# Where the sums of the second weights are formed, and how the last block is stored

## The chip, the cores and the metric

The kernel runs on one core of a Trainium2 chip. The metric is the device time of that core in microseconds, the median of several executions. The engines are named as in the profile: PE (TensorE, matmuls), PEld (its weight loads), DVE (VectorE), ACT (ScalarE), POOL (GpSimd) and SP (SyncE, which here only issues DMAs). Each works through its own instructions in order and waits on semaphores of the others.

## The reference, cut to what matters

A linear attention with a decaying state gives 3072 tokens of 512 numbers. A mixture of experts follows: all 8 experts run on all tokens, and each expert's output is weighted per token by a matrix `P` that 8 rounds of Sinkhorn normalisation make.

```
for e in range(E):                       # 8 experts
    h = np.maximum(x @ w1[e], 0.0)       # 3072x512 @ 512x1024
    ye = h @ w2[e]                       # 3072x1024 @ 1024x512
    out += P[:, e:e + 1] * ye
```

The product `h @ w2[e]` and the sum over the experts are the part that the change touches. It is the last stage of the program, from about 1119 us on.

## The kernel before, in words

The attention comes first, then stage A (`x @ w1`, with relu), then stage B (`h @ w2`). Both products are computed in 2x2 blocks with seven block products instead of eight (Winograd's form of Strassen's scheme). They are named M1 to M7. For seven products, the kernel needs sums of blocks as operands beside the blocks themselves: on the side of `h` stage A has stored them in DRAM (`hd`), on the side of `w2` they are formed in stage B, once per expert.

Every operand is split for precision into a rounded part in float32r and the rest (operand minus rounded part). A block product then takes three matmuls: rounded by rounded, rest by rounded, rounded by rest. ACT makes the rounded part (`hi_act`, L77), DVE makes the rest (`lo`, L80).

**Units and rows.** Stage B has 24 units, `UnitB(n, e, r)`: 8 experts (in falling order) by 3 blocks `r` of 1024 tokens. The list `ROW` sets the order of the block products. One row of the program is: M6 of unit n, M1 of unit n+1, M3 of n, M7 of n, M2 of n+1, M5 of n+1, M4 of n. So M1 is the second product of a row, M2 the fifth, M5 the sixth, M4 the seventh. A product is four parts (`q` = 0 to 3) of six matmuls (`mm`, L551), so a row is 28 parts or 168 matmuls. The rows of one expert are three: its first, its second and its third.

**What a part issues.** `b_part(s)` issues part s: the six matmuls; after a product's last part `post(i)`, which is a copy on ACT (M1, M5, M6; L579) or an output block on DVE (`emit`, for M2, M3, M7, M4: a sum with a stored copy, L562, and a product with `P`, L564; for M4 only the product, L560); then the loads of blocks of `h` that a place has come free for (`h_load`, L611, on SP); then the conversion of the `h` block of part s+5 (`h_conv`: ACT rounds, DVE makes the rest). Since six buffers hold the rounded parts, that conversion waits until PE has left part s-1. The third matmul of a part is the first to read the rest.

**Outputs.** The first expert's blocks are stored by SP (L567). All later ones are added to DRAM by a DMA with `accum_op=ALU.add`, which POOL issues (L569).

**Second weights.** For each change of expert, seven in all, `w2_tasks` prepares the next expert's `w2` in two halves f = 0 and 1. A half is: a load of 1 MB to the buffer `RW` (`w2_load`, L622, on SP); four subtractions 128x512 in that buffer (`tt`, L652, on POOL), which make the operands of M5, M6, M4 and M7; then three times a rounding (`hi`, ACT) and a rest (`rest`, DVE), for 3, 2 and 2 of the seven operands. The results go to the one of the tiles `X0` and `X1` that the running expert does not read. Both halves stand in one list `bq`, filled after the first part of the expert's first row. In three of four parts one entry is taken from it:

```
            if q != 1:
                run(bq, 1)
            if g == 0 and i == M6 and q == 0 and e + 1 < E:
                bq.extend(w2_tasks(e + 1, 0) + w2_tasks(e + 1, 1))
```

So the load of half 0 falls into the row's first product, its four subtractions go to POOL in M3 and M7, and its rests to DVE in M2 and M5. The load of half 1 comes in M4, its subtractions in M1 and M3 of the second row. The new operands are first read in M1 of the third row.

Of the kernel before, what the change touches and what calls it, by code (L numbers as in the profile page):

```python
# [12 lines left out]
ALU = mybir.AluOpType  # L13
# [4 lines left out]
N, DM, E, F = B * S, H * D, 8, 1024  # L18
# [7 lines left out]
NPAIR = CPB // 2  # L26
# [11 lines left out]
M1, M2, M3, M4, M5, M6, M7 = range(7)  # L38
PRE = [M1, M2, M5]
# [4 lines left out]
VP = {M1: 0, M2: 1, M3: 2, M7: 3, M5: 4, M6: 5, M4: 6}  # L44
# [3 lines left out]
def kernel(  # L48
# [17 lines left out]
    pe, act, dve, pool = nc.tensor, nc.scalar, nc.vector, nc.gpsimd  # L66
    sp = nc.sync
# [5 lines left out]
    def rd(t):  # L73
        return t.bitcast(F32)

    def hi_act(o, i):
        act.activation(o, i, AF.Copy)  # L77

    def lo(eng, o, full, h):
        eng.tensor_tensor(o, full, rd(h), ALU.subtract)  # L80
# [23 lines left out]
    def run(q, n):  # L104
        for _ in range(min(n, len(q))):
            q.pop(0)()
# [72 lines left out]
    class UnitA:  # L179
# [22 lines left out]
        def post(self, i):  # L202
            t = self.t
            ps = PS1[self.bank[i]]
            s1, s5, u2, c12 = [TMP[:, k, :] for k in range(4)]
            if i == M1:
                act.activation(s1, ps, AF.Copy)
            elif i == M5:
                act.activation(s5, ps, AF.Copy)
            elif i == M6:  # L210
                act.activation(u2, ps, AF.Copy)
            elif i == M3:
                dve.tensor_tensor(c12, ps, u2, ALU.add)  # L213
                dve.scalar_tensor_tensor(self.new("S3"), c12, 0.0, t["A11"], ALU.max, ALU.subtract)
                self.store("S3", M7)
            elif i == M7:
                o = self.new("A22")
                dve.tensor_tensor(o, ps, s5, ALU.add)  # L218
                act.activation(o, o, AF.Relu)  # L219
                self.store("A22", M4)  # L220
                self.new("S1")
                self.new("S2")
            elif i == M2:
                o = self.new("A11")
                dve.tensor_tensor(o, ps, s1, ALU.add)  # L225
                act.activation(o, o, AF.Relu)  # L226
                self.store("A11", M1)
            elif i == M4:
                act.activation(self.new("A12"), ps, AF.Relu)  # L229
                self.store("A12", M2)  # L230
# [23 lines left out]
    with tc.manual_schedule():  # L254
        with ExitStack() as ph:
# [156 lines left out]
            for tau in range(2, NCHUNK):  # L412
                c, b = divmod(tau, B)
# [107 lines left out]
        def place(s):  # L521
            return HX[s - 8] if 8 <= s < 12 else HL[(s if s < 8 else s - 4) % NHL]

        def follows(s):
            u = s - 4 - NHL
            return u if u < 8 else u + 4
        WB = [X1, X0]
        YS = [OT[:, 10:12, :], XSC[:, 0:2, :], XSC[:, 2:4, :]]
        TB = [OT[:, 2 * k:2 * k + 2, :] for k in range(3)]
        PB = [XSC[:, 2:4, :]] + [OT[:, 6 + 2 * k:8 + 2 * k, :] for k in range(2)]  # L530
        y_n = [0]

        class UnitB:
# [37 lines left out]
            def post(self, i):  # L571
                ps = self.pieces(i)
                s1, s5, u2 = TB
                if self.n == 0:
                    s1 = YS[1]

                def copy(o):
                    for d, t in ps:
                        act.activation(o[:, d], t, AF.Copy)  # L579

                if i == M1:
                    copy(s1)
                elif i == M5:
                    copy(s5)
                elif i == M6:
                    copy(u2)
                elif i == M2:
                    self.emit(0, 0, ps, s1)
                elif i == M3:
                    self.emit(0, 1, ps, u2)  # L590
                elif i == M7:
                    self.emit(1, 1, ps, s5)
                elif i == M4:
                    self.emit(1, 0, ps, None)

            def load_p(self):
                src = pd.rearrange("(e m) s -> e m s", e=E)[self.e, 8 * self.r:8 * self.r + 8, :]
# [3 lines left out]
        UB = [UnitB(n, e, r) for n, (e, r) in enumerate((e, r) for e in reversed(range(E)) for r in range(NPAIR))]  # L601
# [6 lines left out]
        def h_load(s):  # L608
            if s < len(parts):
                u, i, q = parts[s]  # L610
                sp.dma_start(rd(place(s)), hd[u.e][u.r][i][:, q, :])  # L611

        def h_conv(s):
            if s < len(parts):
                hi, low = HH[s % NHH], place(s)
                hi_act(hi, rd(low))
                lo(dve, low, rd(low), hi)

        w2x = RW.rearrange("p (s c) -> p s c", s=7)

        def w2_load(e, f):
            sp.dma_start(w2x[:, 0:4, :], w2[E - 1 - e, f])  # L622
# [15 lines left out]
        w2t = [(M5, M7, M1), (M6, M3, M5), (M4, M2, M6), (M7, M7, M3)]  # L638
# [10 lines left out]

        def w2_tasks(e, f):  # L650
            def tt(o, a, b):
                return lambda: pool.tensor_tensor(w2x[:, VP[o]], w2x[:, VP[a]], w2x[:, VP[b]], ALU.subtract)  # L652

            def hi(a, b):
                t = WB[e % 2][:, a:b, :, f * 512:(f + 1) * 512]
                hi_act(t[:, :, 0], w2x[:, a:b])

            def rest(a, b):
                t = WB[e % 2][:, a:b, :, f * 512:(f + 1) * 512]
                lo(dve, t[:, :, 1], w2x[:, a:b], t[:, :, 0])  # L660

            q = [lambda: w2_load(e, f)] + [lambda: None] * 6
            q += [tt(*x) for x in w2t]
            for a, b in ((0, 3), (3, 5), (5, 7)):
                q += [lambda a=a, b=b: hi(a, b), lambda a=a, b=b: rest(a, b)]
            return q

        bq = []

        nload = [NHL + 4]  # L670

        def b_part(s):
            u, i, q = parts[s]
            if i == M6 and q == 0 and u.n + 1 < len(UB):
                UB[u.n + 1].load_p()
            u.mm(i, q, (HH[s % NHH], place(s)))
            if q == QE - 1:
                u.post(i)
            if s >= 4:
                while follows(nload[0]) <= s:  # L680
                    h_load(nload[0])
                    nload[0] += 1
                h_conv(s + 5)
            e, g = divmod(u.n, NPAIR)
            if q != 1:
                run(bq, 1)
            if g == 0 and i == M6 and q == 0 and e + 1 < E:
                bq.extend(w2_tasks(e + 1, 0) + w2_tasks(e + 1, 1))


        x_load(X1, 1)
# [10 lines left out]
        for n, u in enumerate(UA):  # L702
# [16 lines left out]
            for m, (k, i) in enumerate(ROW):  # L719
                w = (u, v)[k]  # L720
                if w is not None:
                    w.mm(i)
                    w.post(i)
                if m == 0 and carry is not None:
                    carry.last_sum()
                if m == 4:
                    u.sums()
                if m in (0, 1, 5):
                    run(wq, 1)
                if m in (1, 6) or n >= NJ:  # L730
                    run(xq, 2 if n >= NJ else 1)
                for f, x in w2_plan.get((n, m), ()):
                    w2_first(f, x)
                if n == NUA - 2 and m in (5, 6):
                    h_conv(m - 5)
                if n == NUA - 1:
                    for x in {1: (0, 1), 4: (2, 3)}.get(m, ()):
                        b_part(x)
                    for x in {1: (2,), 3: (3,), 4: (4,), 5: (5,)}.get(m, ()):
                        h_conv(x)  # L740
# [8 lines left out]
            h_load(s)  # L749
        for s in range(6, 9):  # L750
            h_conv(s)
        for s in range(4, len(parts)):
            b_part(s)

# [50 lines left out]
```

## Time and profile before

| | |
|---|---|
| median of 3 runs | 2079.45 us (2075.53 to 2083.27) |
| the profiled execution | 2079.61 us |
| its span, first to last instruction | 2077.1 us |
| PE busy | 1992.0 us, 96% of the span |
| DVE busy | 1549.1 us, 75% |
| ACT busy | 1042.0 us, 50% |
| POOL busy | 499.5 us, 24% |
| mean granted TensorE clock | 0.984 |
| stage B: first and last matmul start | 1119.3 and 2066.1 us |

The shares are averages over three stages with different limits. For a change to stage B they say little. What counts there is which wait holds up PE and at what places.

### The profile page before, as it was taken

To read this page: it belongs to the slowest core of one execution; us is meant where nothing else is said; L and a number is where in the kernel's file an instruction comes from. 1 tells how busy PE (TensorE), PEld (TensorE's weight loads), DVE (VectorE), ACT (ScalarE), POOL (GpSimd) and SP (SyncE) were. 2 spreads that over 40 slices of the span, in tenths; PEclk is the share of its full clock that TensorE was granted. 3 is DMA by queue.
4 is the path that set the end of the run, shared out by engine and by line. 5 is a ranking of instruction groups with operands and counts; after the bars stand their busy time and mean duration, and the time that the engine had idled before them with its cause. 6 is when DMAs were issued, how large, how long until landed. Compare 5 with 4: busy or idle time off the path is not lost.

```text
span 2077.1 us, 28831 instructions
## 1 busy us (share of the span) xinstructions
PE 1992.0 (96%) x9273; PEld 1647.7 (79%) x9273; DVE 1549.1 (75%) x2025; ACT 1042.0 (50%) x1668; POOL 499.5 (24%) x479
## 2 busy tenths in 40 slices
PE   7888999998899999999999999999999999999997
PEld 6786877887688888888887887887878787787886
DVE  6795988995666666666677787869687877869765
ACT  3342554553444444444445655555555565555553
POOL 4462433431212111211123101212031112203001
PEclk9898999999999999999999999999999999999999
DMA  7755776776566666666677989999999999999987
GB/s 238 245 168 172 242 247 200 247 249 195 187 216 226 219 221 218 232 214 221 215 248 252 314 269 278 274 276 264 265 293 257 280 275 271 276 284 256 269 266 157
DMA packets 252904, 503.61 MB, mean 242 GB/s; under 512 B 27792, under 2 KB 40400, under 8 KB 250704
## 3 DMA queue, kind: packets, MB, share of 16 engines
q1 hardware_dynamic: 240656, 457.73, 65.5%
q0 software_dynamic: 12096, 44.05, 11.6%
q8 instruction: 72, 1.18, 0.3%
q14 instruction: 80, 0.66, 0.1%
HBM read 268.79 MB, written 232.88 MB: 242 GB/s over the span
## 4 chain that ended last, share of the span: by engine, by line
PE 81%; DVE 6%; issue 5%; DMA 5%; SPq 1%; ACT 1%; POOL 0%; POOLq 0%; DVEq 0%; ACTq 0%
PE psA L190 41%; PE psA L551 21%; PE psB L551 16%; DMA WA<-hd 3%; DVE WA L80 2%; DVE QL L80 1%; PE ps_s L327 1%; SPq L112 1%; DVE X L80 1%; PE ps_x L363 1%; DMA RW<-w 1%; PE psA L372 1%; PE ps_t L339 1%; PE ps_x L358 1%; DVE ta L330 0%
## 5 line engine op out<-in xcount | busy, mean ns | idle before, releaser
L190 PE MATMUL psA<-X,WA 128*128 128x512 f32 x4032 | 932.2, 393 | 23.8 <-DVE OT L213 18.2
L190 PEld LDWEIGHTS psA<-X,WA 128*128 128x128 f32 x4032 | 762.4, 190 | 188.9 <-DVE OT L213 20.3
L551 PE MATMUL psA<-WA,X 128*128 128x512 f32 x2296 | 535.9, 390 | 10.6 <-DVE WA L80 10.1
L77 ACT ACTIVATE WA<-WA 128x512 fp32r<-128x512 f32 x668 | 402.4, 629 | 256.4 <-PE psB L551 109.9
L551 PEld LDWEIGHTS psA<-WA,X 128*128 128x128 f32 x2296 | 429.8, 188 | 106.1 <-DVE WA L80 16.8
L80 DVE TENSOR_TENSOR WA<-WA,WA 128x512 fp32r<-128x512 f32 x487 | 352.3, 767 | 103.4 <-ACT WA L77 97.4
L551 PE MATMUL psB<-WA,X 128*128 128x512 f32 x1728 | 405.1, 390 | 9.1 <-DVE WA L80 6.1
L551 PEld LDWEIGHTS psB<-WA,X 128*128 128x128 f32 x1728 | 324.4, 188 | 79.8 <-DVE WA L80 9.1
L158 POOL TENSOR_TENSOR RW<-RW 128x256 f32<-128x256 f32 x244 | 227.8, 944 | 633.5 <-DMA RW<-w 364.5
L80 DVE TENSOR_TENSOR WA<-RW,WA 128x768 fp32r<-128x768 f32 x122 | 145.3, 1192 | 52.6 <-ACT WA L77 52.3
L219 ACT ACTIVATE OT<-OT 128x512 f32<-128x512 f32 x96 | 60.7, 632 | 244.9 <-DVE OT L218 244.9
L80 DVE TENSOR_TENSOR WA<-WA 128x512 fp32r<-128x512 f32 x181 | 138.8, 794 | 36.9 <-ACT WA L77 35.1
L569 POOL DMA_DIRECT2D out<-XSC x57 | 49.5, 868 | 475.1 <-DVE XSC L564 259.5
L213 DVE TENSOR_TENSOR OT<-psA,OT 128x512 f32<-128x512 f32 x96 | 66.2, 690 | 106.8 <-PE psA L190 106.8
L77 ACT ACTIVATE WA<-RW 128x768 fp32r<-128x768 f32 x122 | 109.4, 946 | 23.0 <-POOL RW L158 13.9
L225 DVE TENSOR_TENSOR OT<-psA,OT 128x512 f32<-128x512 f32 x96 | 66.2, 690 | 59.1 <-ACT OT L219 52.0
L652 POOL TENSOR_TENSOR RW<-RW 128x512 f32<-128x512 f32 x56 | 88.0, 1577 | 60.1 <-DVE WA L80 29.2
L229 ACT ACTIVATE OT<-psA 128x512 f32<-128x512 f32 x96 | 57.4, 598 | 73.6 <-PE psA L190 43.9
L579 ACT ACTIVATE OT<-psA 128x512 f32<-128x512 f32 x96 | 57.4, 598 | 73.2 <-PE psA L551 69.3
L236 DVE TENSOR_TENSOR OT<-OT 128x512 f32<-128x512 f32 x96 | 91.5, 954 | 3.3
L226 ACT ACTIVATE OT<-OT 128x512 f32<-128x512 f32 x96 | 60.7, 633 | 65.3 <-DVE OT L225 65.3
L240 DVE TENSOR_TENSOR OT<-OT 128x512 f32<-128x512 f32 x96 | 70.1, 730 | 30.3 <-ACT OT L229 26.3
(114 smaller groups left out, 1502.3 us busy)
## 6 DMA issues: line engine op xcount, KB each, us to landing
hd<-OT SPq DMA_DIRECT2D x672, 256.0 KB, 2.6
WA<-hd SPq DMA_DIRECT2D x668, 256.0 KB, 6.0
RW<-w SPq DMA_DIRECT2D x61, 512.0 KB, 4.4
out<-XSC POOLq DMA_DIRECT2D x57, 512.0 KB, 8.1
RW<-w SPq DMA_DIRECT2D x16, 1024.0 KB, 8.3
out<-OT POOLq DMA_DIRECT2D x27, 512.0 KB, 8.1
OT<-pd SPq DMA_DIRECT2D x23, 512.0 KB, 7.0
raw<-kT SPq DMA_DIRECT2D x24, 256.0 KB, 3.8
```

The lines of the kernel that those rows point to most:

```text
L77: act.activation(o, i, AF.Copy)
L80: eng.tensor_tensor(o, full, rd(h), ALU.subtract)
L158: eng_add.tensor_tensor(x[:, WP[o]], x[:, WP[p]], x[:, WP[q]], op)
L190: pe.matmul(ps, w[:, a, k * P:(k + 1) * P], x[:, b, k * 512:(k + 1) * 512], start=i in PRE and k == 0 and m == 0, stop=k == 1 and m == 2, ...
L213: dve.tensor_tensor(c12, ps, u2, ALU.add)
L219: act.activation(o, o, AF.Relu)
L225: dve.tensor_tensor(o, ps, s1, ALU.add)
L226: act.activation(o, o, AF.Relu)
L236: dve.tensor_tensor(t["S2"], t["S1"], t["A11"], ALU.subtract)
L240: dve.tensor_tensor(self.new("S4"), self.t["A12"], self.t["S2"], ALU.subtract)
L551: pe.matmul(ps[d] if isinstance(ps, tuple) else ps[:, d, :], w[:, a, q * 256 + d * P:q * 256 + d * P + P], h[b], start=i in PRE and q == 0 ...
L652: return lambda: pool.tensor_tensor(w2x[:, VP[o]], w2x[:, VP[a]], w2x[:, VP[b]], ALU.subtract)
```

## The change

Three things are changed, all in stage B.

- The four subtractions of a half are issued on DVE instead of POOL. One stands behind each part of the second product (M1) of a row: half 0 in the expert's first row, half 1 in the second.
- Roundings and rests no longer come from a list that is emptied entry by entry. They stand at fixed parts: rounding and rest of the first three operands behind the first part of M5, then rounding, rest and rounding behind its other three parts, and the last rest behind the first part of M4. The load of half 1 is issued behind the second part of M4 in the first row, the load of half 0 for the next change of expert behind the first part of the third row; the very first one ahead of the loop.
- The last output block of the program (M4 of the last unit) is not accumulated by POOL. SP loads the running sum of that block to `TB[0]`; DVE multiplies each half by `P` and adds the loaded half; SP stores each half.

```diff
+                elif i == M4 and self.n < len(UB) - 1:
+                    self.emit(1, 0, ps, None)
                 elif i == M4:
-                    self.emit(1, 0, ps, None)
+                    o = out[2 * self.r + 1, 0].rearrange("p (d t) -> p d t", d=2)
+                    sp.dma_start(TB[0], o)
+                    for d in range(2):
+                        y, t = YS[0][:, d], [t for x, t in ps if x.start <= d < x.stop][0]
+                        dve.tensor_tensor(y, t[:, d % t.shape[1]], PB[1 + self.n % 2][:, 1, :], ALU.mult)
+                        dve.tensor_tensor(y, y, TB[0][:, d], ALU.add)
+                        sp.dma_start(o[:, d], y)
...
-                return lambda: pool.tensor_tensor(w2x[:, VP[o]], w2x[:, VP[a]], w2x[:, VP[b]], ALU.subtract)
+                return lambda: dve.tensor_tensor(w2x[:, VP[o]], w2x[:, VP[a]], w2x[:, VP[b]], ALU.subtract)
...
-            q = [lambda: w2_load(e, f)] + [lambda: None] * 6
-            q += [tt(*x) for x in w2t]
-            for a, b in ((0, 3), (3, 5), (5, 7)):
-                q += [lambda a=a, b=b: hi(a, b), lambda a=a, b=b: rest(a, b)]
-            return q
+            t = [tt(*x) for x in w2t]
+            h = [lambda a=a, b=b: hi(a, b) for a, b in ((0, 3), (3, 5), (5, 7))]
+            r = [lambda a=a, b=b: rest(a, b) for a, b in ((0, 3), (3, 5), (5, 7))]
+            return {(f, M1, x): [t[x]] for x in range(4)} | {
+                (f, M5, 0): [h[0], r[0]], (f, M5, 1): [h[1]], (f, M5, 2): [r[1]], (f, M5, 3): [h[2]],
+                (f, M4, 0): [r[2]]}
...
-            e, g = divmod(u.n, NPAIR)
-            if q != 1:
-                run(bq, 1)
-            if g == 0 and i == M6 and q == 0 and e + 1 < E:
-                bq.extend(w2_tasks(e + 1, 0) + w2_tasks(e + 1, 1))
+            e, g = divmod(u.n - (i in PRE), NPAIR)
+            if u.n >= (i in PRE) and e + 1 < E:
+                if (g, i, q) == (0, M6, 0):
+                    w2p.clear()
+                    w2p.update(w2_tasks(e + 1, 0) | w2_tasks(e + 1, 1))
+                for f in w2p.get((g, i, q), ()):
+                    f()
+                if (g, i, q) == (0, M4, 1):
+                    w2_load(e + 1, 1)
+                if (g, i, q) == (2, M6, 0) and e + 2 < E:
+                    w2_load(e + 2, 0)
...
+        w2_load(1, 0)
         for s in range(4, len(parts)):
             b_part(s)
```

On DVE, this is the difference in the second product of an expert's first row (here the second expert's; `WA` tiles hold blocks of `h`, `RW` the loaded weights; L661 is the subtraction's line in the changed kernel):

```order
-L80 TENSOR_TENSOR WA0_71<-WA0_71,WA2_1774 128x512 x3
-L80 TENSOR_TENSOR WA0_71<-WA0_71,WA1_72 128x512
+L80 TENSOR_TENSOR WA0_71<-WA0_71,WA2_1774 128x512
+L661 TENSOR_TENSOR RW_73<-RW_73 128x512
+L80 TENSOR_TENSOR WA0_71<-WA0_71,WA2_1774 128x512
+L661 TENSOR_TENSOR RW_73<-RW_73 128x512
+L80 TENSOR_TENSOR WA0_71<-WA0_71,WA2_1774 128x512
+L661 TENSOR_TENSOR RW_73<-RW_73 128x512
+L80 TENSOR_TENSOR WA0_71<-WA0_71,WA1_72 128x512
+L661 TENSOR_TENSOR RW_73<-RW_73 128x512
```

The four subtractions now stand one by one between the rests of four parts of `h`; on POOL they are gone, and only the accumulating stores are left there.

On DVE in the fifth to seventh product of the same row (`X1` is the tile that takes the next expert's operands, L562 and L564 are the output block of M2):

```order
+L562 TENSOR_TENSOR OT_1775<-psB1_4774,OT_1775 128x1024
+L564 TENSOR_TENSOR OT_1775<-OT_1775 128x1024
+L80 TENSOR_TENSOR WA0_71<-WA0_71,WA1_72 128x512 x2
 L80 TENSOR_TENSOR X1_1773<-RW_73,X1_1773 128x3x512
-L562 TENSOR_TENSOR OT_1775<-psB1_4774,OT_1775 128x1024
-L564 TENSOR_TENSOR OT_1775<-OT_1775 128x1024
-L80 TENSOR_TENSOR WA0_71<-WA0_71,WA1_72 128x512 x2
+L80 TENSOR_TENSOR WA0_71<-WA0_71,WA1_72 128x512
+L80 TENSOR_TENSOR WA0_71<-WA0_71,WA2_1774 128x512
 L80 TENSOR_TENSOR X1_1773<-RW_73,X1_1773 128x2x512
-L80 TENSOR_TENSOR WA0_71<-WA0_71,WA1_72 128x512
-L80 TENSOR_TENSOR WA0_71<-WA0_71,WA2_1774 128x512
```

The three rests of the weights (to `X1`) moved behind M2's output block and behind two more rests of `h`.

On DVE at the end of the program (`psA` holds M4 of the last unit):

```order
 L562 TENSOR_TENSOR XSC_74<-psA1_254,OT_1775 128x512
 L564 TENSOR_TENSOR XSC_74<-XSC_74,OT_1775 128x1024
-L560 TENSOR_TENSOR XSC_74<-psA0_253,OT_1775 128x512
-L560 TENSOR_TENSOR XSC_74<-psA1_254,OT_1775 128x512
+L601 TENSOR_TENSOR OT_1775<-psA0_253,OT_1775 128x512
+L602 TENSOR_TENSOR OT_1775<-OT_1775 128x512
+L601 TENSOR_TENSOR OT_1775<-psA1_254,OT_1775 128x512
+L602 TENSOR_TENSOR OT_1775<-OT_1775 128x512
```

Two instructions became four. On SP's queue a load of `out` stands behind the last load of `h`, and two stores behind it.

## Rows read from the trace of the kernel before

**Rows 1.** Waits in stage B: engine and line <- releaser: us, times, longest.

```profile
POOL RW L652 <- DMA RW<-w: 28.7, 7, 22.4
PEld psA L551 <- DVE WA L80: 16.8, 15, 1.9
PE psA L551 <- DVE WA L80: 10.1, 13, 1.5
PEld psB L551 <- DVE WA L80: 5.9, 4, 1.9
PE psB L551 <- DVE WA L80: 4.5, 3, 1.5
```

**Rows 2.** Windows: stretch, length, PE busy (x matmuls), clock, DMA share, GB/s.

```profile
1186.00:1256.00 70.00, 70.00 (x311) 1.00 0.86 287
1256.00:1304.00 48.00, 45.46 (x199) 1.00 0.94 264
...
1846.00:1894.00 48.00, 45.54 (x198) 1.00 0.96 272
```

**Rows 3.** Timeline, a first row: start, us, engine, instructions [idle before <- releaser].

```profile
1281.22 2.55 DVE L80 TENSOR_TENSOR WA<-WA 128x512 fp32r<-128x512 f32 x1
...
1281.58 5.04 POOL L652 TENSOR_TENSOR RW<-RW 128x512 f32<-128x512 f32 x3
...
1283.69 3.48 DVE L80 TENSOR_TENSOR WA<-WA,WA 128x512 fp32r<-128x512 f32 x2
...
1289.55 4.35 DVE L80 TENSOR_TENSOR WA<-WA,WA 128x512 fp32r<-128x512 f32 x4
...
1290.29 1.66 PE L551 MATMUL psA<-WA,X 128*128 128x512 f32 x6 [0.24 <-DVE WA L80]
1290.54 1.59 POOL L652 TENSOR_TENSOR RW<-RW 128x512 f32<-128x512 f32 x1
...
1292.74 4.38 PE L551 MATMUL psA<-WA,X 128*128 128x512 f32 x18 [0.80 <-DVE WA L80]
...
1293.82 1.75 DVE L80 TENSOR_TENSOR X<-RW,X 128x1536 fp32r<-128x1536 f32 x1
...
1298.61 3.70 PE L551 MATMUL psA<-WA,X 128*128 128x512 f32 x15 [1.49 <-DVE WA L80]
```

**Rows 4.** Timeline of a third row, without work on weights.

```profile
1348.61 1.29 DVE L80 TENSOR_TENSOR WA<-WA 128x512 fp32r<-128x512 f32 x2 [2.74 <-ACT WA L77]
...
1369.02 11.04 PE L551 MATMUL psA<-WA,X 128*128 128x512 f32 x48
...
1370.48 1.23 DVE L564 TENSOR_TENSOR XSC<-XSC,OT 128x1024 f32<-128x1024 f32 x1
1371.62 2.49 DVE L80 TENSOR_TENSOR WA<-WA,WA 128x512 fp32r<-128x512 f32 x4
...
1375.81 2.70 DVE L80 TENSOR_TENSOR WA<-WA,WA 128x512 fp32r<-128x512 f32 x4 [1.70 <-ACT WA L77]
...
1379.90 4.47 PE L551 MATMUL psB<-WA,X 128*128 128x512 f32 x19
```

**Rows 5.** Timeline of DVE in a second row, beside POOL's subtractions.

```profile
1310.95 4.83 DVE L80 TENSOR_TENSOR WA<-WA,WA 128x512 fp32r<-128x512 f32 x4 [2.31 <-ACT WA L77]
```

**Rows 6.** The loads of the second weights, L622.

```profile
DMA to landing us min/median/max: 5.8/8.3/10.4
```

**Rows 7.** Timeline of the program's end.

```profile
2062.87 0.86 POOL L569 DMA_DIRECT2D out<-XSC  x1 [4.58 <-DVE XSC L564]
2065.88 1.37 DVE L560 TENSOR_TENSOR XSC<-psA,OT 128x512 f32<-128x512 f32 x2 [3.31 <-PE psA L551]
2067.55 0.86 POOL L569 DMA_DIRECT2D out<-XSC  x1 [3.81 <-DVE XSC L560]
```

**Rows 8.** Landings of POOL's accumulating stores, L569.

```profile
DMA to landing us min/median/max: 5.3/8.1/10.6
```

**Rows 9.** The page's DMA issues: count, KB each, us to landing.

```profile
hd<-OT SPq DMA_DIRECT2D x672, 256.0 KB, 2.6
```

More of the change, by code (lines that the diff above doesn't have):

```diff
@@ L660, in rest @@
                 lo(dve, t[:, :, 1], w2x[:, a:b], t[:, :, 0])
-            q = [lambda: w2_load(e, f)] + [lambda: None] * 6
-            q += [tt(*x) for x in w2t]
-            for a, b in ((0, 3), (3, 5), (5, 7)):
-                q += [lambda a=a, b=b: hi(a, b), lambda a=a, b=b: rest(a, b)]
-            return q
-        bq = []
+            t = [tt(*x) for x in w2t]
[4 more added lines that the diff above has]
+                (f, M4, 0): [r[2]]}
+        w2p = {}
         nload = [NHL + 4]
```

## The prediction

> **What bounds the kernel now.** I read the waits of stage B first. PE waits there for one thing only, DVE's line 80, the rests: 10.1 + 4.5 us in 16 waits, and its weight loads for the same line 16.8 + 5.9 us [rows 1]. So DVE is late at some places; where, the windows show. In 70 us between two changes of expert PE is busy throughout (311 matmuls, clock 1.00). In 48 us around a change it has 199, and in the last such window 198 [rows 2]; six windows look like this, the changes to the third up to the eighth expert. The change to the second shows no loss. A window's count includes a cut matmul at either edge, so the full rate is 309 in 70 us, 4.41 per us; 48 us would hold 212, and 197 or 196 are there. Some 15 are missing, at 0.227 us each 3.4 us per change, about 20 us in six. The waits bracket this: PE's own idle time, 14.6 us, leaves out what slow starts cost, and that of the weight loads, 22.7 us, counts some that hides.
>
> The timeline of a first row tells why DVE is late [rows 3]. A single rest takes 2.55 us at 1281.22, two take 3.48 and four 4.35, each time while POOL subtracts beside it. In a quiet row four rests take 2.49 us, 0.60 each and 0.08 at the end [rows 4]. So one, two and four should take 0.69, 1.29 and 2.49: POOL's four subtractions cost DVE 1.86 + 2.19 + 1.86 = 5.9 us. They fall into M3, M7 and M2, and the weights' rests (1.75 us the first) into the same stretch. PE then restarts after DVE at 1290.29, 1292.74 and 1298.61. In second rows POOL's subtractions stretch four rests to 4.83 us as well, but DVE had waited 2.31 us for ACT just before [rows 5], and PE loses nothing. The stretching does harm only where DVE has no time left.
>
> **The change, part by part.** Of the profiled execution's 2079.61 us, 2.5 lie outside its span; the median of the runs shown is 2079.45, so no correction is made.
>
> The subtractions leave POOL. 56 go (four for each of 14 halves), and with them the stretching of rests, 5.9 us on DVE in each first row.
>
> They come to DVE. Two inputs in the buffer and 128x512 results are the form of a rest, so 0.60 us each in a queue, 2.4 us per row, 34 us of DVE in 14 rows. They stand in M1, where DVE runs out of work: its first two rests of that stretch wait 2.74 us for ACT [rows 4]. What hides the 2.4 us is this idle time and the lead of the rests. If that cover were gone, 2.4 us per row would go to PE. Below nothing they can't cost, since POOL's share is counted above. From 0 to 2.4 us per row I take 0.
>
> Rests of the weights, in M5 and M4. I lay them into the quiet row [rows 4]. M5 begins at 1369.02, with four parts of 1.36 us, so M4 begins at 1374.46, and its part k needs its rest at 1374.9 + 1.36k (third matmul). M2's output block ends at 1371.7. In the new order follow: the rests for M4's first two parts, done at 1372.3 and 1372.9 (needed 1374.9, 1376.3); the first rest of the weights, 1.7 us, to 1374.6; two rests of M4, to 1375.3 and 1375.9 (needed 1377.6, 1379.0); the second of the weights, 1.2 us as the 128x1024 product at 1370.48, to 1377.1; two rests of the next row, at 1377.7 and 1378.3 (needed 1380.3, 1381.7); the third, to 1379.5; two more at 1380.1 and 1380.7 (needed 1383.0, 1384.4). The least lead is 2.3 us, so PE never waits. If each weight rest cost twice as much the lead would be used up; that bounds the cost at about 2 us per row, below nothing it can't be. I take 0.
>
> So the six stalls go: 20 us, from 14.6 to 22.7. What is late next is DVE again, with 2.3 us to spare.
>
> The loads. SP issues 1 MB in M4's second part once the last weight rest is done, 1379.5 in the quiet row. All loads of `h` behind it on SP wait with it for that rest, as they did before, since that load stood behind a weight rest in M4 already. It lands 5.8 to 10.4 us after issue, median 8.3 [rows 6], so between 1385.3 and 1389.9. The first subtraction's turn on DVE comes 8.1 us into a row (1348.61 + 1.29, where the row began 38.08 us before 1379.90, at 1341.82), thus at 1388.0. DVE waits 0 to 1.9 us for the load, at a place where the rests behind it lead by more than that. Before, POOL did this waiting: seven waits for the load [rows 1]. I take 0. The other load moves two parts of a row ahead by a whole row, away from the first, which spreads the traffic; the DMA share around changes is 0.94 to 0.96 and 0.86 in the window between [rows 2]. From 0 to 2 us per change if it were late, I take 0. The load ahead of the loop goes against loads of `h` at the stage's start: 0 to 3 us (a third of its 8.3), once; I take 0, since its subtractions come a whole product and more later.
>
> The last block. Now DVE starts on it at 2065.88, POOL issues at 2067.55 [rows 7], the store lands 5.3 us later (the least value of its line, with nothing else under way) at 2072.9 [rows 8], and the span ends at 2077.1, 4.2 us after. New: two instructions per half at 0.69 us give halves at 2067.3 and 2068.7. A store of 256 KB by SP takes 2.6 us [rows 9], so the second lands at 2071.3. The load of the running sum has no waiter ahead of it on SP and lands during the last products. POOL's last store is then M7's, issued at 2062.87; it lands at 2068.2 and would with the same 4.2 us let the span end at 2072.4. The end lies between 2071.3 (no tail behind SP's store) and 2075.5 (the same tail behind it): a gain of 1.6 to 5.8 us. I take 4.5, by POOL's branch, since POOL's closing work follows POOL's own last store.
>
> Sum: 2079.6 - 20 - 4.5 = 2055.1 us; predicted 2055. With the terms' ends 2051 to 2064.
>
> **The rivals.**
>
> DVE too full (slower). Place: the second product of 14 rows. If DVE's idle time there isn't real cover, the 2.4 us moved onto it reach PE in each of them: 14 x 2.4 = 34 us. The old stalls stay, only the end gains: 2079.6 + 34 - 4.5 = 2109. It decides once the rests behind M1 lead by less than 2.4 us. For it: every wait of PE is for DVE. Against: 2.74 and 2.31 us of idle time right there [rows 4, 5], and POOL's stretching by 2.3 us was borne at that place without loss.
> The Trainium skill (Perfetto Trace Analysis, "Optimizing Scalar/DVE Operations") would move work the other way: with DVE saturated, work may be handed to ScalarE or even GPSIMD. By that rule this change is a step back and this rival would come out; the same section adds that between GPSIMD and DVE it may not help because of a shared read port, and the stretched rests [rows 3] agree with the addition.
>
> DVE waits for the second load (slower or same). Place: first subtraction of the second row. If a load took over 12 us, the wait would pass 3.6 us and eat the lead; from about 15 us on, with 3.5 us or more lost in each of seven rows, the gain is gone: 2079 and over. Against: the longest of 16 was 10.4 us [rows 6].
>
> The DMA engines set the pace. If 117.6 us per expert were what the traffic needs, PE's freed time would turn into waits for `h`, and only the end would gain: 2075. For it: shares of 0.94 and 0.96 around changes. Against: PE runs 70 us at a stretch without a wait, at 287 GB/s [rows 2].
>
> Half of the stalls stay, because the weights' rests and not POOL make up part of them: 2065. For it: the longest stop, at 1298.61, comes behind the rests of the weights. Against: second rows have the same rests and no stops.
>
> **How the numbers follow.** Forecast 0.80, at 2055 with its own range 2050 to 2061; half of the stalls 0.06; DMA pace 0.06; load wait 0.03; DVE too full 0.05. What can be told from no change by measuring is about 0.5%, 10.4 us: under 2069 is faster. Faster 0.86 (forecast and half), same 0.08 (DMA pace, part of the load's), slower 0.06. The range 2050 to 2064 holds the forecast with its terms' ends; the cases outside it are 0.2.
>
> **What would show it.** In the profile after, PE should have no wait for line 80 from 1150 us to its end, and 48 us around a change should hold 212 or 213 matmuls. All single rests should take about 0.69 us, none 1.8 or 2.5. DVE's busy time should hardly rise: 34 us come, and more than 35 of stretching in six first rows go. POOL should show accumulating stores alone in stage B, and the time from the last matmul to the span's end should fall from some 11 to some 6 us. It is wrong if PE waits for DVE in M1 or M3 (too full), if DVE waits for the load of the weights, or if ACT waits for `h`.

## The result, and the profile after

The changed kernel takes 2054.69 us (median of 5 runs, 2050.62 to 2057.07) against 2079.55 us before (5 runs): a ratio of 0.9875, 95% interval 0.9854 to 0.9895. Forecast were 2055 us, so 24.9 us less came against 24.5 predicted. The interval reaches from 21.8 to 30.4 us less, so that the two agree to half a microsecond is partly luck; the single terms below test the forecast better. The profiled execution's span fell from 2077.1 to 2051.8 us. The engines' busy time, from its page:

```profile
PE 1985.9 (97%) x9273; PEld 1647.2 (80%) x9273; DVE 1527.7 (74%) x2083; ACT 1041.7 (51%) x1668; POOL 406.0 (20%) x422
```

DVE has 58 instructions more than before (2083 against 2025) and 21.4 us less of busy time (1549.1 before); POOL has 57 fewer and 93.5 us less.

The waits of stage B hold no row for PE or its weight loads any more (1150 to 2030 us), where there were 16 and 19 waits for line 80 [rows 1]. The windows that answer to [rows 2] (stretch, length, PE busy and its matmuls, clock, DMA share, GB/s):

```profile
1256.00:1304.00 48.00, 48.00 (x213) 1.00 0.92 274
...
1374.00:1422.00 48.00, 48.00 (x214) 1.00 0.93 283
1846.00:1894.00 48.00, 48.00 (x213) 1.00 0.90 270
```

The 14 or 15 matmuls that each window lacked are back. Three rows, which is one expert, now take 114.2 us at every change, where the six slow ones took 117.6. Now the two places on DVE, in the first row of the same expert as in [rows 3]. First M1, where the subtractions went (start, us, engine, instructions, idle time before and what ended it):

```profile
1268.69 1.29 DVE L80 TENSOR_TENSOR WA<-WA,WA 128x512 fp32r<-128x512 f32 x2 [2.74 <-ACT WA L77]
1269.90 0.68 DVE L661 TENSOR_TENSOR RW<-RW 128x512 f32<-128x512 f32 x1
...
1270.50 0.68 DVE L80 TENSOR_TENSOR WA<-WA,WA 128x512 fp32r<-128x512 f32 x1
...
1274.55 0.69 DVE L80 TENSOR_TENSOR WA<-WA,WA 128x512 fp32r<-128x512 f32 x1 [1.56 <-ACT WA L77]
1275.16 0.69 DVE L661 TENSOR_TENSOR RW<-RW 128x512 f32<-128x512 f32 x1
```

DVE's instructions start 0.60 us after one another, and it still waits for ACT ahead of the first subtraction and again ahead of the fourth. Then M5 and M4, with PE's row of M5:

```profile
1289.10 11.04 PE L551 MATMUL psA<-WA,X 128*128 128x512 f32 x48
...
1290.56 1.22 DVE L564 TENSOR_TENSOR OT<-OT 128x1024 f32<-128x1024 f32 x1
...
1291.70 1.28 DVE L80 TENSOR_TENSOR WA<-WA,WA 128x512 fp32r<-128x512 f32 x2
...
1292.91 1.75 DVE L80 TENSOR_TENSOR X<-RW,X 128x1536 fp32r<-128x1536 f32 x1
...
1294.58 1.29 DVE L80 TENSOR_TENSOR WA<-WA,WA 128x512 fp32r<-128x512 f32 x2
...
1295.78 1.22 DVE L80 TENSOR_TENSOR X<-RW,X 128x1024 fp32r<-128x1024 f32 x1
...
1296.92 1.28 DVE L80 TENSOR_TENSOR WA<-WA,WA 128x512 fp32r<-128x512 f32 x2
```

M4's third part has its third matmul at 1289.10 + 6 x 1.36 + 0.45 = 1297.7. Its rest is the first of the two at 1294.58 and ends at 1295.26: 2.45 us ahead. That is the least lead of any rest in all first and second rows, read off the trace part by part (rest's end against the third matmul's start). Before, it was 0.05 us in first rows, which is a stop, and 0.41 in second rows.

The end, to [rows 7]:

```profile
2042.27 0.86 POOL L569 DMA_DIRECT2D out<-XSC  x1 [4.58 <-DVE XSC L564]
2045.22 0.69 DVE L601 TENSOR_TENSOR OT<-psA,OT 128x512 f32<-128x512 f32 x1 [3.25 <-PE psA L551]
2045.94 0.69 DVE L602 TENSOR_TENSOR OT<-OT 128x512 f32<-128x512 f32 x1
2046.55 0.68 DVE L601 TENSOR_TENSOR OT<-psA,OT 128x512 f32<-128x512 f32 x1
2046.66 1.66 SPq L603 DMA_DIRECT2D out<-OT  x2
2047.27 0.69 DVE L602 TENSOR_TENSOR OT<-OT 128x512 f32<-128x512 f32 x1
```

The last matmul starts at 2045.5, so 6.4 us pass to the end of the span, instead of 11.0.

Where the 25.3 us of span went follows from matmul starts. The profiled executions of kernels with the same stage A differ by up to 7.5 us in when stage B begins (1117.2 to 1124.7 us; 1119.3 and 1119.1 in the two compared here), so I count from its ninth part (1142.55 us before, 1142.22 after), from which on PE runs without the join of the stages. From there to the span's end were 934.6 us and are 909.6. Between the starts of two matmuls that don't wait 0.227 us pass. Pauses of over 0.06 us beyond that sum to 20.3 us in this stretch before and 0.4 after, so 19.8 went; the end gave 4.6, and the last 0.5 lie in pauses too short to count. The 0.4 us left stand in the last unit, behind an output block (L562), in both kernels.

### The profile page after: what moved, and what is told of

The parts are those of the page before. It is cut to its first block, busy times and chain, and to the rows that moved or that the text cites. A ratio compares the mean times of both kernels' runs of the same rounds, so it can differ in the third digit from the quotient of the medians.

```text
span 2051.8 us, 28824 instructions
## 1 busy us (share of the span) xinstructions
PE 1985.9 (97%) x9273; PEld 1647.2 (80%) x9273; DVE 1527.7 (74%) x2083; ACT 1041.7 (51%) x1668; POOL 406.0 (20%) x422
## 4 chain that ended last, share of the span: by engine, by line
PE 90%; DVE 4%; DMA 3%; issue 1%; ACT 1%; SPq 1%; POOL 0%; DVEq 0%; ACTq 0%
PE psA L190 42%; PE psA L551 25%; PE psB L551 19%; DMA raw<-kT 1%; DVE QL L80 1%; PE ps_s L327 1%; PE ps_x L363 1%; DMA RW<-w 1%; PE psA L372 1%; PE ps_x L358 0%; PE ps_t L339 0%; DVE X L80 0%; DVE ta L330 0%; SPq L112 0%; DMA hd<-OT 0%
## 5 line engine op out<-in xcount | busy, mean ns | idle before, releaser
L80 DVE TENSOR_TENSOR WA<-WA,WA 128x512 fp32r<-128x512 f32 x487 | 313.7, 685 | 99.4 <-ACT WA L77 94.9
L158 POOL TENSOR_TENSOR RW<-RW 128x256 f32<-128x256 f32 x244 | 220.8, 915 | 637.9 <-DMA RW<-w 412.8
L569 POOL DMA_DIRECT2D out<-XSC x56 | 48.5, 865 | 611.7 <-DVE XSC L564 365.6
L80 DVE TENSOR_TENSOR WA<-WA 128x512 fp32r<-128x512 f32 x181 | 121.7, 697 | 35.4 <-ACT WA L77 34.4
L229 ACT ACTIVATE OT<-psA 128x512 f32<-128x512 f32 x96 | 57.5, 599 | 77.1 <-PE psA L190 40.3
L579 ACT ACTIVATE OT<-psA 128x512 f32<-128x512 f32 x96 | 57.4, 598 | 72.7 <-PE psA L551 68.8
L211 ACT ACTIVATE OT<-psA 128x512 f32<-128x512 f32 x96 | 57.4, 598 | 64.0 <-PE psA L190 63.9
```

The costliest lines, as they stand in the source:

```text
L158: eng_add.tensor_tensor(x[:, WP[o]], x[:, WP[p]], x[:, WP[q]], op)
```

## The experiments

Time and ratio to the kernel before are from 4 to 10 runs of each kernel and 7 to 13 of the kernel before on the same chip. The ratio is not the quotient of the two medians and can differ from it slightly. Leads (how long a rest ends ahead of the matmul that needs it) and pauses are read off the trace for every part.

**Only the engine** (the kernel before, subtractions on DVE at their old places).

```diff
-  return lambda: pool.tensor_tensor(w2x[:, VP[o]], w2x[:, VP[a]], w2x[:, VP[b]], ALU.subtract)
+  return lambda: dve.tensor_tensor(w2x[:, VP[o]], w2x[:, VP[a]], w2x[:, VP[b]], ALU.subtract)
```

> The kernel before with one word changed: the four subtractions of a half are on DVE, at their old places (in M3 and M7 for half 0), the rests of the weights at their old places too, the last block as before. Theory (POOL stretches DVE's rests where DVE has no time left): in first rows 5.9 us of stretching go and 2.4 us of subtractions come, so DVE is 3.5 us earlier where PE lost 3.4 us; the stops shrink to 0 to 1 us per change and the time is 2060 to 2066 us. Rival (it was the places of the rests that mattered): the stops stay near 3.4 us per change, less 1 at most, and the time is 2074 to 2080 us.

Measured: 2059.93 us, ratio 0.9902 (0.9884 to 0.9921). No rest is stretched and first rows have no stop; their least lead is 0.27 us. Stops of 0.2 to 0.7 us appear in second rows, at M4's first part, 3.5 us in seven, where the expectation had not looked. DVE and PE there:

```profile
1213.12 1.22 DVE L80 TENSOR_TENSOR X<-RW,X 128x1024 fp32r<-128x1024 f32 x1
...
1214.26 1.22 DVE L562 TENSOR_TENSOR XSC<-psB,OT 128x1024 f32<-128x1024 f32 x1
1215.51 1.22 DVE L564 TENSOR_TENSOR XSC<-XSC,OT 128x1024 f32<-128x1024 f32 x1
...
1216.65 1.29 DVE L80 TENSOR_TENSOR WA<-WA,WA 128x512 fp32r<-128x512 f32 x2
...
1217.39 4.87 PE L551 MATMUL psA<-WA,X 128*128 128x512 f32 x20 [0.43 <-DVE WA L80]
```

M2's output block and, ahead of it, a rest of the weights stand before the rest that M4 needs. So the engine alone removes 16.4 of the 19.8 us of stopping, though DVE gets more instructions; the old places leave it next to no lead. The time came out just under the expected range, and the rival falls.

**Only the places** (the changed kernel, subtractions back on POOL; the edit is the one above, reversed).

> The changed kernel with the subtractions back on POOL, at the new places in M1. Theory: POOL stretches rests by 2 to 5 us again, but in M1, where DVE waits for ACT anyway, so PE loses nothing and the time is that of the changed kernel, 2053 to 2058 us. Rival (the engine alone decides): the stops come back with the stretching, 3 us per change or more, in 6 to 14 rows: 2073 us or more.

Measured: 2052.65 us, ratio 0.9865 (0.9846 to 0.9884); from the ninth part to the end 909.6 us, as in the changed kernel. PE has no wait in stage B. 50 rests are stretched, by 53.5 us in all (56.6 before):

```profile
1251.84 6.71 DVE L80 TENSOR_TENSOR WA<-WA,WA 128x512 fp32r<-128x512 f32 x4
...
1252.99 6.71 POOL L661 TENSOR_TENSOR RW<-RW 128x512 f32<-128x512 f32 x4
...
1254.67 5.60 PE L551 MATMUL psB<-WA,X 128*128 128x512 f32 x24
...
1258.47 2.38 DVE L80 TENSOR_TENSOR WA<-WA 128x512 fp32r<-128x512 f32 x2
```

The waits came as expected and the time 0.35 us under the range; the place came only in part: where the load had long landed, nothing held POOL until M1, and 20 of the 56 subtractions ran one to three products earlier. The lines show four of them, in M5 and M4 of the third row before; the least lead, behind them, was 0.32 us. So the places alone are enough too, by a small margin. The rival, that the engine decides, falls.

**Only the last block** (the kernel before with the new branch for M4 of the last unit).

> The kernel before with the last block alone stored by halves. Theory: the time from the last matmul's start to the end of the span falls from 11.0 to about 6.3 us and nothing else changes; the time is 2074 to 2076 us. Rival (the end is hidden behind something else, or the load of the running sum delays SP's loads): no change at the end, 2079 to 2080 us.

Measured: 2075.29 us, ratio 0.9981 (0.9967 to 0.9996). From the last matmul's start (2070.58) to the end of the span (2076.95) 6.4 us, as in the changed kernel, and the stops of first rows are all there (with one more, of 1.0 us, at the change to the second expert). The term stands by itself; the time alone, 0.8 to 6.9 us less, would bound it only loosely.

**Four more subtractions on DVE, in M1.** The second of the four is written once more and the third three times more, with the same result (the expectation says three of them; it is two):

```diff
-  return {(f, M1, x): [t[x]] for x in range(4)} | {
+  return {(f, M1, x): [t[x]] * (1, 2, 4, 1)[x] for x in range(4)} | {
```

> The changed kernel with eight subtractions per half on DVE instead of four (three of them written again with the same result), all in M1, in 14 rows. Theory: the 2.4 us more per row are taken from DVE's idle time and its lead in M1; PE has no wait, the time is that of the changed kernel within 2 us. Rival (DVE is too full for added work): 14 x 2.4 = 34 us more, 2088 us.

Measured: 2053.95 us, ratio 0.9873 (0.9856 to 0.9889), no wait of PE. The least lead fell to 1.71 us, behind M1 in M7 and M2. Work added on DVE at this place cost nothing.

**Eight more** (factors 3, 4, 4, 1).

> The changed kernel with twelve subtractions per half on DVE in M1 instead of four (three of them written several times with the same result). With four more the least lead of a rest in those rows was 1.71 us, behind M1 in M7 and M2; 2.4 us more per row exceed it by 0.7. Theory: PE now stops, 0.3 to 1 us in each of 14 rows, at M7 or M2; time 2059 to 2069 us. Rival (DVE's load as such is the price): 14 x 4.8 = 67 us over the changed kernel, 2122 us.

Measured: 2069.08 us, ratio 0.9961 (0.9946 to 0.9976), just above the expected range. PE stops in each of the 14 rows at M7's first part, by turns 1.3 and 0.9 us, 15.5 us together:

```profile
1276.98 2.87 DVE L661 TENSOR_TENSOR RW<-RW 128x512 f32<-128x512 f32 x4
...
1279.76 0.69 DVE L80 TENSOR_TENSOR WA<-WA,WA 128x512 fp32r<-128x512 f32 x1
1280.36 2.87 DVE L661 TENSOR_TENSOR RW<-RW 128x512 f32<-128x512 f32 x4
...
1283.15 0.68 DVE L80 TENSOR_TENSOR WA<-WA,WA 128x512 fp32r<-128x512 f32 x1
...
1283.89 5.28 PE L551 MATMUL psA<-WA,X 128*128 128x512 f32 x22 [0.63 <-DVE WA L80]
```

The first 2.4 us per row were free, of the second 2.4 about 1.1 were paid. So the rival of a full DVE has its point between four and eight more instructions; the change is well on the free side.

**POOL reading again.** The changed kernel with four subtractions more on POOL at the old places of first rows, which write to a tile that nobody reads:

```diff
+  if (g, i, q) in ((0, M3, 3), (0, M7, 0), (0, M7, 2), (0, M7, 3)):
+      pool.tensor_tensor(SCR, w2x[:, 0], w2x[:, 1], ALU.subtract)
```

> The changed kernel with four subtractions more on POOL, at the old places in M3 and M7 of first rows; they read the weights' buffer and write to a tile that nobody reads, so nothing waits for them. Theory: DVE's rests beside them take 1.8 to 2.5 us again, 5.9 us more in each first row against a lead of 2.45: stops of 2.5 to 3.5 us in six or seven rows; time 2070 to 2080 us. Rival (the stops came from the chain subtraction, rounding, rest, so from waiting for POOL's results): no stop, 2053 to 2057 us.

Measured: 2064.59 us, ratio 0.9939 (0.9924 to 0.9954), 10 us over the changed kernel where 15 or more were expected. The stretching is back as in [rows 3], and PE stops in M5 (PE waits for DVE at 1293.67 and 1296.14):

```profile
1284.61 2.55 DVE L80 TENSOR_TENSOR WA<-WA 128x512 fp32r<-128x512 f32 x1
...
1284.97 5.03 POOL L703 TENSOR_TENSOR SCR<-RW 128x512 f32<-128x512 f32 x3
...
1287.08 3.48 DVE L80 TENSOR_TENSOR WA<-WA,WA 128x512 fp32r<-128x512 f32 x2
...
1293.67 1.66 PE L552 MATMUL psA<-WA,X 128*128 128x512 f32 x6 [0.24 <-DVE WA L80]
...
1296.14 4.14 PE L552 MATMUL psA<-WA,X 128*128 128x512 f32 x17 [0.81 <-DVE WA L80]
```

The pauses add up to 1.6 us in M5, and in M4 to some 0.2, where the kernel before lost another 1.8 (its restart at 1298.61 in [rows 3]). So the stop in M5 comes from the stretching alone: nothing waits for these subtractions. The stop in M4 needed the stretching and the weights' rests at their old places together: with the engine alone changed, the rests at their old places stop no first row, and here, with the rests moved, the stretching hardly does so in M4. My expectation had subtracted 5.9 us from the least lead of 2.45 as if both fell at one place; the least lead is in M4, while the rests in M2 and M5, where the stretching falls, lead by 3.1 and more.

**POOL only writing.** The same four places, with zeros filled in:

```diff
-      pool.tensor_tensor(SCR, w2x[:, 0], w2x[:, 1], ALU.subtract)
+      pool.memset(SCR, 0.0)
```

> As the run with four subtractions more on POOL, but POOL only fills the tile with zeros: it writes and reads nothing. If the stretching comes from POOL reading the buffer beside DVE's two inputs, no rest takes over 0.7 us and the time is that of the changed kernel, 2053 to 2057 us. If any work of POOL stretches them, rests of 1 us and more are back and PE stops in first rows: 2060 to 2080 us.

Measured: 2053.79 us, ratio 0.9886 (0.9870 to 0.9903), no wait of PE. POOL's row, then DVE's (count, then least, median and greatest ns):

```profile
L703 POOL MEMSET SCR<- x28: 519/529/867, 1133.4 to 1858.6; 128x512 f32 x28
```

```profile
L80 DVE TENSOR_TENSOR WA<-WA,WA x487: 681/686/699, 1131.6 to 2036.7; 128x512 fp32r<-128x512 f32 x163
```

A MEMSET is shorter than a subtraction (0.53 against 1.6 us), but 30 rests overlapped one and took 0.69 us at most, while in the run before this 27 rests overlapped the 28 subtractions and took 0.98 to 2.55 us, every one of them lengthened.

**The last two blocks.** M7 of the last unit also stored by halves from SP, its running sum loaded ahead:

```diff
+  elif i == M7:
+      o = out[2 * self.r + 1, 1].rearrange("p (d t) -> p d t", d=2)
+      sp.dma_start(TB[2], o)
+      sp.dma_start(TB[0], out[2 * self.r + 1, 0].rearrange("p (d t) -> p d t", d=2))
...
+          dve.tensor_tensor(y, y, PB[1 + self.n % 2][:, 1, :], ALU.mult)
+          dve.tensor_tensor(y, y, TB[2][:, d], ALU.add)
+          sp.dma_start(o[:, d], y)
```

> The changed kernel with the last unit's M7 block stored by halves from SP as well, so that POOL's last store is that of M3, 5.4 us earlier. Theory: the end of the span follows the later of two tails, POOL's closing work 8.8 us after its last store's issue began and SP's last landing; with POOL's out of the way the span ends about 1 us sooner after the last matmul's start, 5.3 us instead of 6.4. Rival (the tail follows the last landing whoever issued it): no change, 6.4 us.

Measured: 2054.11 us, ratio 0.9888 (0.9874 to 0.9903). From the last matmul's start to the end 6.1 us: 0.25 less, of 1.0 expected. POOL's store was out of the way (its closing drain ended at 2051.9 us of 2056.1), but then SP's last landing, at 2054.5, and its own closing waits, to 2055.4, came last. In the changed kernel SP's closing waits were through at 2050.14, 0.94 us ahead of POOL's drain; at most that much could be gained. Here they took 0.8 us behind the landing instead of 0.15, and most of it went. Why they took longer is open. Neither theory was right in size, and the tail of 8.8 us behind POOL's last issue is no constant: here it was 10.6.

**The same step for the first expert's weights**, which are prepared while stage A ends. Its second half goes to DVE (condition `f == 1`), in the second run both halves:

```diff
-  pool.tensor_tensor(w2x[:, VP[o]], w2x[:, VP[a]], w2x[:, VP[b]], ALU.subtract)
+  (pool if f == 0 else dve).tensor_tensor(w2x[:, VP[o]], w2x[:, VP[a]], w2x[:, VP[b]], ALU.subtract)
...
-  lo(dve if i % 2 == 0 else pool, t[:, 1], w2x[:, VP[i]], t[:, 0])
+  lo(dve if i % 2 == 0 or f == 1 else pool, t[:, 1], w2x[:, VP[i]], t[:, 0])
```

> The changed kernel with the same step taken for the first expert's second half of weights, which is prepared while stage A ends: its four subtractions and three rests go from POOL to DVE. Theory: DVE's instructions of 1.8 us at the join of the stages (1118 to 1128 us) go back to 0.7, the stops of PE there (2.2 and 2.7 us of some 12) shrink, and from the first matmul of stage B to its ninth part take 18 to 22 us instead of 23.1; time 2050 to 2054 us. Rival (DVE is fuller there than anywhere, so seven more instructions of 0.6 us are 4 us more on the path): 24 to 27 us, 2056 to 2060 us.

> As the run before it, with both halves of the first expert's weights on DVE. Theory: the first half's share stands in stage A, where POOL's three rests and four subtractions stretch DVE less at places where PE waits; 0 to 2 us beside the run with one half, 2049 to 2055 us. Rival (seven more on DVE in stage A stop PE there, which waits for DVE's sums already): 4 us more, 2055 to 2060 us.

Measured: 2052.87 us, ratio 0.9864 (0.9849 to 0.9879), and 2055.01 us, ratio 0.9866 (0.9846 to 0.9886). The intervals overlap with that of the changed kernel, so neither is shown to be better. DVE's instructions at the join, 1.75 to 1.78 us between 1118 and 1127 us in the changed kernel, take 0.69, and from stage B's first matmul to its ninth part 19.4 us pass in both, instead of 23.1, as expected. In stage A, just before, PE now waits 1.2 us for DVE's sums (L218) and in the second run 1.6 us more for ACT. The local gain is shown, the net one stays open.

## Why the prediction was right, point by point

**What bounds the kernel.** Right. PE was stopped by late rests alone. "POOL's four subtractions cost DVE 1.86 + 2.19 + 1.86 = 5.9 us" stands: the run with POOL reading again brings the same durations back in a kernel that had none. The place was misread ("They fall into M3, M7 and M2"): issued in M3 and M7, the 28 subtractions of first rows ran 1 in M3, 15 in M7, 6 in M2 and 6 in M5. What I had not seen either is that the full 3.4 us per change needed two things, the stretching and the early weights' rests. The stretching alone, with the rests moved, still costs half (10.3 us of 20, nearly all of it in M5); the early rests without it, though DVE then had the subtractions too, cost nothing in first rows and 3.5 us in second ones. With rests and subtractions both moved, almost as much stretching (53.5 us against 56.6) cost nothing.

**The subtractions on DVE, taken as 0.** Right, and with a margin: four more are free, eight more are not. The stated range, though, held only the ends of the two gains; what the terms taken as 0 could cost (2.4 us per row here) was left to the rivals.

**The rests in M5 and M4, "the least lead is 2.3 us".** Measured 2.45, at the place named (M4's third part). Laying the new order by hand into a row of the old trace was accurate to 0.15 us, since the chain held only instructions whose durations the trace had.

**The stalls, 20 us (14.6 to 22.7).** Measured 19.8. Of the three ways to count, that by missing matmuls (20.6 in six windows) came closest; PE's idle time in the waits (14.6) is too small, since the pauses between matmul starts hold more than it.

**The loads, taken as 0.** Right. The slowest took 11.0 us, a little over the 10.4 known before; PE does not show it.

```profile
DMA to landing us min/median/max: 5.9/7.7/11.0
```

**The last block, 4.5 us (1.6 to 5.8).** Measured 4.6, by the branch that I took (its own sum, 2077.1 - 2072.4, is 4.7): by the trace's record of POOL's DRAIN, which the views leave out, its closing drain ran 8.84 us from 2042.24 to 2051.08, as it had run 8.83 us from 2067.53 before. SP's halves landed earlier than I had them, in 2.0 us instead of 2.6, and made no difference.

**The rivals.** DVE too full: false here, and its point is now known. The Trainium skill's advice to move work off a saturated DVE (Perfetto Trace Analysis, "Optimizing Scalar/DVE Operations") did not apply, since DVE was busy for 75% of the span. Its remark that a move between DVE and GpSimd may not help agrees with the runs: with 56 subtractions more in stage B DVE's busy time fell, and with the subtractions back on POOL at the new places the time was that of the changed kernel. The load: no wait of DVE for it in the changed kernel. DMA pace: the share around changes is 0.90 to 0.94 with PE running through, and an expert takes 114.2 us, so the traffic did not need 117.6. Half of the stalls: no stop was left, though its premise was sound: the weights' rests had their part in M4's stop. The change moves them too. One size was off: I wrote that DVE's busy time would hardly rise, and it fell by the 21.4 us above, because the stretching in second rows went as well (56.6 us of it in all rows, against 34 us of new work). One sign that I had named as showing it wrong did come: ACT waits for `h`, three times and 4.5 us in all between 1142 and 1152 us, where it waited 1.7 us before. The load now put ahead of the loop may be the reason (1.4 to 1.7 us in the three runs without it, 1.2 to 5.4 in those with it); PE has no wait there, so the sign was badly chosen.

## What to carry to other kernels

Before moving work between two engines, count what each slows the other by: here a POOL subtraction of 1.6 us cost DVE 1.1 us, and doing it on DVE took 0.6. An engine that PE waits for may still have free time at other places of the same loop; lay the new order into a row of the trace and compare each result's time with the matmul that needs it. When one remedy seems to explain a gain, try the others alone: of the stops, the places alone would have removed all and the engine alone 16.4 of 19.8 us.

## What the runs showed of the hardware

A DVE instruction with two inputs in SBUF took 1.78 us instead of 0.69 beside a POOL subtraction, some 2.5 where the subtraction followed POOL's issue of a store, and 0.69 beside a POOL MEMSET. Beside POOL's issue of a store alone it took 0.69 as well (233 rests of the changed kernel). The Trainium skill (SBUF — State Buffer, "Who interferes with whom") says that such a DVE instruction contends with a GpSimd instruction that reads SBUF and not with one that only writes it; the two runs agree.

POOL's closing drain ended 3.4 to 3.5 us after its last accumulating store had landed in every profile here; from that store's issue it took 8.7 to 8.9 us, but 10.6 in the run with the last two blocks, where the landing took 7.2 us instead of 5.2 to 5.4. SP's stores of 256 KB at the program's end landed in 2.0 us.
